# Attention and FFN on one core: VectorE's share of the exponentials as three shifted int16 readings summed by weighted copies of V

## The chip, the cores and the metric

The kernel runs on one core of a Trainium2 chip. Five engines work from queues of their own: PE (TensorE, matmuls), ACT (ScalarE), DVE (VectorE), POOL (GpSimd) and SP (SyncE, which issues DMAs). They meet through semaphores. The metric is the time of one execution in microseconds (us); the kernel before takes 813.2 us, the median of 3 runs between 810.48 and 814.16.

## The reference

```python
xn = layernorm(x)                                   # x: 1 x 2048 x 640
q = (xn @ wq).reshape(1, 2048, 32, 20)              # 32 heads of 20
k, v = xn @ wk, xn @ wv                             # one k and one v for all heads: 2048 x 20
p = softmax(einsum("bhqd,bkd->bhqk", q, k) * 20 ** -0.5)
o = einsum("bhqk,bkd->bhqd", p, v)
out = x + o.reshape(1, 2048, 640) @ wo + silu(xn @ w1) @ w2     # w1: 640 x 1728
```

All is bf16. The 32 x 2048 x 2048 scores need 134 million exponentials; that is the bulk of the work of the engines beside PE.

## The kernel before

**Units, groups, steps.** A unit is one head and one chunk of 512 queries: 128 units. Three units make a group (the last has two), 43 groups. A group takes 16 steps, one for each tile of 128 keys: 688 steps. In step t, `do_S` issues the scores S: three matmuls of 128 keys x 512 queries, side by side in three row tiles of PE (a head has only 20 dimensions), into three PSUM banks. Two sets of three banks alternate, so S of step t+2 waits until the exponentials of step t have been read out. One score block of 512 columns per unit and step is exponentiated:

- ACT takes two or three blocks in one `ACTIVATE` (L735, `exp`).
- In some steps (`want_dve`) DVE takes the third block. The scores come from PE already scaled and offset, so that their integer value is a bf16 bit pattern: `p1` (L749) clamps them and writes int16, Z. Read as bf16, this bit pattern is an exponential that is linear between powers of two. Every four blocks `flush_z` corrects them by three operations over up to 2048 columns: `u` (L800) takes the mantissa, `T1` (L803) multiplies it with Z into Y, `B` (L804) keeps Z's exponent.

The output product P.V follows (`pfn`, L759): 128 keys x 32 columns of V (20 of V, one of ones for the softmax's denominator) against the 512 queries of each unit, in column tiles 0, 1 and 2 of PE side by side. In a DVE step tile 2 takes Y (L765) and tile 3 takes Z (L767); both sums are combined later. At a group's end DVE copies the sums U out of PSUM in fp32r (`Uev`, L821), PE transposes them against a 0/1 matrix `stk` that also adds the tiles up (`UT`, L827), and DVE divides by the denominators (`rcp`, `nrm`).

**Other work** is cut into jobs and put between the steps: q of the next chunk (`q_job`, L867), the FFN's first product (`h_job`, L893, with a tanh on ACT, L901, and a product on DVE, L906), transposes of the attention output (`oT_job`), and the FFN's second product with the output projection (`out_job`: L957 against W2, L962 against wo). In the last chunk the W2 part is made ahead (`dst="yx"`), and the wo part stands behind the last group.

**What sets the order.** The program plans itself while it is built: `Sched.run` and `step` keep an expected time for every engine, and pick for PE a score step, a P.V step or a job matmul; the result is a fixed order for each engine. Where PE is expected to be empty, `fill` puts in matmuls with zeros (L635, L641, L654). `want_dve` gives DVE a block if its backlog is below `DVE_TH`. Changing the numbers changes the whole order.

**The head.** Up to about 60 us x is loaded, normalised (`norm`, into `xn`) and transposed; k, v and the first q are made. `v_job` writes V to SBUF once for four key tiles (L1295). POOL prepares constants.

Of the kernel before, what the change touches and what calls it, by code (L numbers as in the profile page):

```python
# [9 lines left out]
F32R = mybir.dt.float32r  # L10
# [5 lines left out]
P = 128  # L16
# [23 lines left out]
OFF_LO = 53.0  # L40
# [5 lines left out]
ZB = 4  # L46
# [3 lines left out]
PV_PRESS = 9  # L50
DVE_TH = 4.0
# [274 lines left out]
class Builder:  # L326
# [17 lines left out]
    def alloc(self):  # L344
        sb = self.sb
        self.ps = self.stack.enter_context(self.nc.psum_tensor("psall", [P, 8 * BANK], F32))
        self.xnT = sb([P, DC, S], BF16)
        self.w1 = sb([P, DC, F], BF16)
        self.w2 = sb([P, FC, D], BF16)
        self.wq = sb([P, DC, HT * P], BF16)  # L350
        self.wo = sb([P, DC, D], BF16)
        self.kv_st = sb([P, 2, DC, DH], BF16)
        self.wk = sb([P, DC, P], BF16)
        self.kT = sb([P, 2, S], BF16)
        self.v = sb([P, KT, SLOT], BF16)
# [5 lines left out]
        self.stk = sb([P, 64], F32R)  # L361
# [157 lines left out]
    def step(self, now):  # L519
# [17 lines left out]
        for op in list(self.pv_q)[:4]:  # L537
# [3 lines left out]
            if op.kt < KT and self.pro_left:  # L541
# [35 lines left out]
        if choice == "PV":  # L577
            head = self.pv_q[0]
            d = (0.216 if head.mode == "PV" else 0.5) + self.switch(head.mode)
# [4 lines left out]
        if choice == "PV":  # L584
# [4 lines left out]
            op.work = 0.216  # L589
# [108 lines left out]
    def do_S(self, t, now):  # L698
# [55 lines left out]

        def pfn(pe):
            ins = None
            for j in range(na):
                q = j if j < nh - 1 else 2
                ins = pe.matmul(self.bk(UBANK, 0, QW, q * SLOT, (q + 1) * SLOT), self.v[:, kt, :],  # L759
                                self.E[:, (b0 + j) * QW:(b0 + j + 1) * QW],  # L760
                                start=first, stop=last, tile_position=(0, q * SLOT))
            if dv:
                y = self.Y[:, zs, zp * QW:(zp + 1) * QW].bitcast(BF16)
                z = self.Z[:, zs, zp * QW:(zp + 1) * QW].bitcast(BF16)
                pe.matmul(self.bk(UBANK, 0, QW, 64, 96), self.v[:, kt, :], y, start=first, stop=last,  # L765
                          tile_position=(0, 64))
                ins = pe.matmul(self.bk(UBANK, 0, QW, 96, 128), self.v[:, kt, :], z, start=(gd == 0),  # L767
                                stop=(self.last_dve_kt[g] == kt), tile_position=(0, 96))
# [3 lines left out]
        pv.mm = na + (2 if dv else 0)  # L772
# [16 lines left out]

    def flush_z(self):  # L790
# [5 lines left out]
        yk = [("Y", zs, i) for i in range(n)]  # L796
        Z = self.Z[:, zs, 0:n * QW]
        Y = self.Y[:, zs, 0:n * QW]
        w = n * QW
        sc.new("dve", t_dve_4x(w), lambda v: v.tensor_scalar(Y, Z, 0x7F, 0x3F80, ALU.bitwise_and, ALU.bitwise_or),  # L800
               zk, yk, prio=4.0, name="u")
        yb, zb = Y.bitcast(BF16), Z.bitcast(BF16)
        sc.new("dve", t_dve_2x(w), lambda v: v.tensor_tensor(yb, zb, yb, ALU.mult), zk + yk, yk, prio=4.0, name="T1")  # L803
        sc.new("dve", t_dve_4x(w), lambda v: v.tensor_scalar(Z, Z, 0x7F80, None, ALU.bitwise_and), zk, zk, prio=4.0,  # L804
               name="B")
        for i, (t, pv) in enumerate(self.zblocks):
            ks = [("Z", zs, i), ("Y", zs, i)]
            pv.deps |= sc.deps_of(ks, ())
            for k in ks:
                sc.readers[k].append(pv)  # L810
        self.zblocks = []

    def end_group(self, g):
# [16 lines left out]
        op = sc.new("pe", 0.5, ut, [("U", up), ("stk",)], [("UB",)], name=f"UT{g}", mode="M", queue=False)  # L830
# [214 lines left out]
    def prologue(self):  # L1045
# [16 lines left out]
        def load_w(eng, key, pieces, tag, nb):  # L1062
            deps = sc.deps_of((), [tag])
# [26 lines left out]
        load_w("sp", "2", w2p, ("w2",), P * D * 2)  # L1090
# [13 lines left out]
        for a, b_, kk in ((0, 4, 0), (4, 32, 1)):  # L1104
            def padset(g, a=a, b_=b_):
# [15 lines left out]
        pool(0.4, lambda g: g.memset(self.v[:, :, :], 0.0), [], [("v0",)] + [("v", i) for i in range(8)])  # L1121
        pool(0.2, lambda g: g.memset(self.v[:, :, DH:DH + 1], 1.0), [("v0",)],
             [("v0",)] + [("v", i) for i in range(8)])
        wqd = self.wq[:, :, :].rearrange("p c (h j) -> p c h j", j=SLOT)
        wqs = self.wq_st.rearrange("p c (h d) -> p c h d", d=DH)
        pool(0.2, lambda g: g.memset(self.stk[:, :].bitcast(F32), 0.0), [], [("stk",)])
# [3 lines left out]
        self.s21 = self.sb([P, 21], F32)  # L1130
        pool(0.15, lambda g: g.tensor_scalar(self.s21[:, :], self.idf[:, 96:117], 2.0, 0.0, ALU.mult, ALU.add),
             [("idf",)], [("s21",)])
        pool(0.15, lambda g: g.tensor_tensor(self.stk[:, 42:63], self.idf[:, 64:85], self.s21[:, :], ALU.add),
             [("s21",), ("idf",)], [("stk",)])
# [105 lines left out]
        def tr_job(n):  # L1240
# [8 lines left out]
            def consume(b):  # L1249
# [32 lines left out]
        def v_job(n0, n1):  # L1282
# [10 lines left out]
            def consume(b):  # L1293
                sv = self.bk(b, 0, 20 * m).rearrange("p (i d) -> p i d", d=DH)
                sc.new("dve", 0.07 + m * 0.025, lambda v: v.tensor_copy(self.v[:, n0:n1, 0:DH], sv), [("B", b)],  # L1295
                       [(kk, i) for i in range(n0 // 2, n1 // 2) for kk in ("v", "vv")], prio=0.6, name=f"vev{n0}")
# [82 lines left out]
```

## Time and profile before

| | us |
|---|---|
| runs, median of 3 | 813.2 (810.48 to 814.16) |
| the profiled execution | 810.35 |
| its span, first to last instruction | 808.6 |
| mean granted PE clock | 0.99 of full speed |
| instructions | 16175 |

The profile shows the one execution. Its busy times are shares of the span; a group of instructions is one line of the kernel, with its count, its busy time, the mean time of one, and the idle time just ahead of it. Records of one engine can overlap by their start-up, so a mean is somewhat longer than the busy time divided by the count. On PE several tiles work at the same time, and a matmul's record is longer than the distance to the next.

### The profile page before, as it was taken

Reading aid. Unit: us, or ns where it says so; the run is one execution under the profiler, and the core shown is the slowest. Engines: PE = TensorE matmul, PEld = TensorE weight load, DVE = VectorE, ACT = ScalarE, POOL = GpSimd, SP = SyncE. Lnnn points to the kernel's source line nnn. Section 1 sums busy time; section 2 is a strip of 40 time slices with the busy share of each in tenths; the row PEclk is TensorE's granted clock in tenths of the full one; section 3 lists DMA queues with packets and bytes.
Section 4 is the critical chain, followed back from the end, with each engine's and each line's share of the span. In section 5 each row is a group of like instructions: output and inputs, shape, how many; then the busy total and the mean of one; then the engine's idle time right before and its main releaser. Section 6 shows DMA issues by size and latency. Waiting matters only on the chain.

```text
span 808.6 us, 16175 instructions
## 1 busy us (share of the span) xinstructions
PE 756.7 (94%) x6398; PEld 268.9 (33%) x6457; DVE 757.4 (94%) x1286; ACT 756.3 (94%) x776; POOL 25.0 (3%) x69
## 2 busy tenths in 40 slices
PE   8889999899999999999999999998989999999995
PEld 4432232223233333223333433322323333333343
DVE  7439999999999999999999999999999999999996
ACT  6989999999999999999999999999999999999850
POOL 4700000000000000000000000000000000000000
PEclk9999999999999999999999999999999999999999
DMA  9500000000000000000000001000000010000000
GB/s 291 176 1 1 2 2 1 2 1 1 1 2 17 19 17 17 2 1 1 2 1 1 18 17 34 1 1 1 2 1 2 17 34 18 1 1 2 1 2 33
DMA packets 13067, 15.02 MB, mean 19 GB/s; under 512 B 3200, under 2 KB 12352, under 8 KB 12992
## 3 DMA queue, kind: packets, MB, share of 16 engines
q1 hardware_dynamic: 11680, 13.93, 5.3%
q8 instruction: 52, 0.85, 0.4%
q10 hardware_dynamic: 1312, 0.05, 0.1%
q14 instruction: 23, 0.19, 0.1%
HBM read 11.36 MB, written 2.62 MB: 17 GB/s over the span
## 4 chain that ended last, share of the span: by engine, by line
PE 42%; DVE 25%; ACT 23%; issue 6%; POOL 1%; DMA 0%; DVEq 0%; ACTq 0%; POOLq 0%
ACT sbt L735 21%; PE psall L717 13%; DVE sbt L749 10%; PE psall L759 10%; PE psall L957 8%; DVE sbt L803 5%; PE psall L962 2%; DVE sbt L800 2%; PE psall L893 2%; ACT sbt L901 2%; DVE sbt L804 2%; PE psall L827 2%; PE psall L641 1%; DVE sbt L906 1%; PE psall L867 1%
## 5 line engine op out<-in xcount | busy, mean ns | idle before, releaser
L735 ACT ACTIVATE sbt<-psall 128x1024 bf16<-128x1024 f32 (+2 forms) x688 | 724.1, 1196 | 24.8 <-PE psall L717 22.0
L749 DVE TENSOR_SCALAR sbt<-psall 128x512 int16<-128x512 f32 x499 | 333.3, 684 | 10.9 <-PE psall L717 9.3
L717 PE MATMUL psall<-sbt 32*128 32x512 bf16 x2048 | 269.6, 386 | 27.1 <-ACT sbt L735 18.3
L759 PE MATMUL psall<-sbt 128*32 128x512 bf16 x1549 | 200.7, 386 | 2.7 <-DVE sbt L856 1.0
L765 PE MATMUL psall<-sbt 128*32 128x512 bf16 x499 | 155.8, 384 | 0.0
L803 DVE TENSOR_TENSOR sbt<-sbt 128x2048 bf16<-128x2048 bf16 (+3 forms) x140 | 153.9, 1102 | 0.8
L717 PEld LDWEIGHTS psall<-sbt 32*128 32x128 bf16 x2048 | 69.5, 91 | 248.4 <-ACT sbt L735 104.6
L767 PE MATMUL psall<-sbt 128*32 128x512 bf16 x499 | 149.5, 384 | 0.0
L800 DVE TENSOR_SCALAR sbt<-sbt 128x2048 int16<-128x2048 int16 (+3 forms) x140 | 87.2, 629 | 1.2
L804 DVE TENSOR_SCALAR sbt<-sbt 128x2048 int16<-128x2048 int16 (+3 forms) x140 | 87.6, 627 | 0.2
L957 PE MATMUL psall<-sbt 128*128 128x320 bf16 x448 | 87.0, 303 | 0.3 <-DVE sbt L971 0.2
L759 PEld LDWEIGHTS psall<-sbt 128*32 128x32 bf16 x1549 | 53.5, 95 | 87.3 <-issue 46.2
L893 PE MATMUL psall<-sbt 128*128 128x512 bf16 (+1 forms) x245 | 78.4, 395 | 3.8 <-issue 2.9
L641 PE MATMUL psall<-sbt 128*32 128x512 bf16 (+8 forms) x190 | 53.7, 355 | 0.0
L957 PEld LDWEIGHTS psall<-sbt 128*128 128x128 bf16 x448 | 35.6, 97 | 45.3 <-issue 30.9
L867 PE MATMUL psall<-sbt 128*128 128x512 bf16 x142 | 43.6, 384 | 3.4 <-issue 1.0
L654 PE MATMUL psall<-sbt 128*128 128x512 bf16 (+6 forms) x156 | 42.6, 385 | 3.2 <-POOL sbt L1101 1.4
L906 DVE SCALAR_TENSOR_TENSOR sbt<-sbt,psall 128x512 bf16<-128x512 bf16 (+1 forms) x56 | 38.3, 683 | 2.0 <-ACT sbt L901 1.3
L901 ACT ACTIVATE sbt<-psall 128x512 bf16<-128x512 f32 (+1 forms) x56 | 38.8, 694 | 0.0
L765 PEld LDWEIGHTS psall<-sbt 128*32 128x32 bf16 x499 | 38.2, 95 | 0.0
L767 PEld LDWEIGHTS psall<-sbt 128*32 128x32 bf16 x499 | 35.4, 94 | 0.1
L962 PE MATMUL psall<-sbt 128*128 128x320 bf16 x160 | 30.8, 302 | 2.8 <-DVE sbt L924 2.1
(87 smaller groups left out, 349.1 us busy)
## 6 DMA issues: line engine op xcount, KB each, us to landing
sbt<-in_A_x_dram SPq DMA_DIRECT2D x32, 160.0 KB, 2.8
out_dram<-sbt SPq DMA_DIRECT2D x16, 160.0 KB, 1.8
sbt<-in_B_w_dram SPq DMA_DIRECT2D x5, 432.0 KB, 6.3
sbt<-in_B_w_dram SPq DMA_DIRECT2D x13, 160.0 KB, 4.6
sbt<-in_A_wo_dram SPq DMA_DIRECT2D x5, 160.0 KB, 6.2
sbt<-in_A_wq_dram SPq DMA_DIRECT2D x5, 140.0 KB, 3.5
sbt<-in_A_wq_dram SPq DMA_DIRECT2D x1, 100.0 KB, 3.5
sbt<-in_B_w_dram SPq DMA_DIRECT2D x1, 80.0 KB, 4.5
```

The source lines that it names most:

```text
L641: return pe.matmul(self.bk(UBANK, 0, n, 0, 32), self.zero[:, 0:32], self.zero[:, 0:n], start=False, stop=False, tile_position=(0, 0), skip ...
L717: ins = pe.matmul(self.bk(par3 + j), self.kT[r:r + SLOT, kk, kt * P:(kt + 1) * P], self.qT[r:r + SLOT, h // 4, (x // H) % 2, :], start=Tru ...
L735: return a.activation(self.E[:, b0 * QW:(b0 + na) * QW], self.ps[:, par3 * BANK:(par3 + na) * BANK], AF.Exp, scale=ACT_SCALE)
L749: return v.tensor_scalar(self.Z[:, zs, zp * QW:(zp + 1) * QW], self.bk(bb), 0.0, ZMAX, ALU.max, ALU.min)
L759: ins = pe.matmul(self.bk(UBANK, 0, QW, q * SLOT, (q + 1) * SLOT), self.v[:, kt, :], self.E[:, (b0 + j) * QW:(b0 + j + 1) * QW], start=fir ...
L765: pe.matmul(self.bk(UBANK, 0, QW, 64, 96), self.v[:, kt, :], y, start=first, stop=last, tile_position=(0, 64))
L767: ins = pe.matmul(self.bk(UBANK, 0, QW, 96, 128), self.v[:, kt, :], z, start=(gd == 0), stop=(self.last_dve_kt[g] == kt), tile_position=(0 ...
L800: sc.new("dve", t_dve_4x(w), lambda v: v.tensor_scalar(Y, Z, 0x7F, 0x3F80, ALU.bitwise_and, ALU.bitwise_or), zk, yk, prio=4.0, name="u")
L803: sc.new("dve", t_dve_2x(w), lambda v: v.tensor_tensor(yb, zb, yb, ALU.mult), zk + yk, yk, prio=4.0, name="T1")
L804: sc.new("dve", t_dve_4x(w), lambda v: v.tensor_scalar(Z, Z, 0x7F80, None, ALU.bitwise_and), zk, zk, prio=4.0, name="B")
L893: return pe.matmul(self.bk(b, 0, QW, 0, rows), self.w1[:, k, fk * P:fk * P + rows], self.xnT[:, k, c * QW:(c + 1) * QW], start=(k == 0), s ...
L957: return pe.matmul(self.bk(b, 0, 320), self.hT[0:rows, fk, i * P:(i + 1) * P], self.w2[0:rows, fk, e0:e0 + 320], start=(m == 0), stop=(m = ...
```

## The change

The three flush operations give way to two additions: `y0 = Z + 43` and `y1 = Z + 86` in int16 (`PH` holds the shifts and weights). Z, y0 and y1, all read as bf16, are multiplied with copies of V scaled by 1, 0.805 and 0.625, and PSUM sums the three. V is kept in five forms: three weights, and the third weight once more in two halves that fit into the free columns of tiles 0 and 1. A DVE step's P.V slot takes two ACT blocks, z in tile 2 and y0 in tile 3. The third readings y1 are collected in steps of their own, named PT, up to three blocks to a slot (tiles 2, 3, and 0 with 1). Three blocks make a flush instead of four (`ZB`), and `DVE_TH` and `PV_PRESS` have new values. U is written in bf16 and transposed in bf16. W2's tile now also holds `xn`, so W2's load waits until the transposes have read `xn`.

```diff
-OFF_LO = 53.0
+OFF_LO = 45.0
+PH = ((0, 1.0), (43, 0.8046875), (86, 0.625))
-ZB = 4
+ZB = 3
-PV_PRESS = 9
-DVE_TH = 4.0
+PV_PRESS = 12
+DVE_TH = 2.6
@@ alloc
-        self.v = sb([P, KT, SLOT], BF16)
+        self.v = sb([P, 5, KT, SLOT], BF16)
-        self.Y = sb([P, NZ, ZB * QW], I16)
-        self.U = sb([P, 2, QW], F32R)
+        self.Y = sb([P, NZ, 2, ZB * QW], I16)
+        self.U = sb([P, 2, QW], BF16)
-        self.xn = sb([P, 4, D], BF16)
+        self.xn = self.w2[:, 0:4, :]
@@ do_S, pfn
             if dv:
-                pe.matmul(self.bk(UBANK, 0, QW, 64, 96), self.v[:, kt, :], y, start=first, stop=last,
-                          tile_position=(0, 64))
-                ins = pe.matmul(self.bk(UBANK, 0, QW, 96, 128), self.v[:, kt, :], z, start=(gd == 0),
-                                stop=(self.last_dve_kt[g] == kt), tile_position=(0, 96))
+                self.pv_mm(pe, 2, 0, kt, z, first, last)
+                ins = self.pv_mm(pe, 3, 1, kt, y, gd == 0, False)
@@ flush_z
-        sc.new("dve", t_dve_4x(w), lambda v: v.tensor_scalar(Y, Z, 0x7F, 0x3F80, ALU.bitwise_and, ALU.bitwise_or),
-               zk, yk, prio=4.0, name="u")
-        yb, zb = Y.bitcast(BF16), Z.bitcast(BF16)
-        sc.new("dve", t_dve_2x(w), lambda v: v.tensor_tensor(yb, zb, yb, ALU.mult), zk + yk, yk, prio=4.0, name="T1")
-        sc.new("dve", t_dve_4x(w), lambda v: v.tensor_scalar(Z, Z, 0x7F80, None, ALU.bitwise_and), zk, zk, prio=4.0,
-               name="B")
+        for k in range(2):
+            sc.new("dve", t_dve_4x(w), lambda v, k=k: v.tensor_scalar(
+                self.Y[:, zs, k, 0:n * QW], Z, float(PH[k + 1][0]), None, ALU.add), zk,
+                [("Y", zs, k, i) for i in range(n)], prio=4.0 + 0.1 * k, name=f"y{k}")
...
+            def th(pe, q, x=x, kt=kt):
+                if q >= 2:
+                    return self.pv_mm(pe, q, 2, kt, x, False, False)
+                self.pv_mm(pe, 0, 3, kt, x, False, False)
+                return self.pv_mm(pe, 1, 4, kt, x, False, False)
...
+            def fn(pe, part=part):
+                ins = None
+                for q, x in zip((2, 3, 0), part):
+                    ins = x[0](pe, q)
+                return ins
+            op = sc.new("pe", 0.3, fn, [x[1] for x in part], [], name="PT", mode="PV", queue=False)
@@ end_group
-        op = sc.new("pe", 0.5, ut, [("U", up), ("stk",)], [("UB",)], name=f"UT{g}", mode="M", queue=False)
+        op = sc.new("pe", 0.28, ut, [("U", up), ("stk",)], [("UB",)], name=f"UT{g}", mode="M", queue=False)
@@ prologue
-        load_w("sp", "2", w2p, ("w2",), P * D * 2)
+        def load_w2():
+            load_w("sp", "2", w2p, ("w2",), P * D * 2, [("xn", i) for i in range(4)])
-        pool(0.4, lambda g: g.memset(self.v[:, :, :], 0.0), [], [("v0",)] + [("v", i) for i in range(8)])
+        pool(0.9, lambda g: g.memset(self.v[:, :, :, :], 0.0), [], [("v0",)] + [("v", i) for i in range(8)])
...
@@ tr_job, consume
+                if n == NT - 1:
+                    load_w2()
@@ v_job, consume
-                sc.new("dve", 0.07 + m * 0.025, lambda v: v.tensor_copy(self.v[:, n0:n1, 0:DH], sv), [("B", b)],
-                       [(kk, i) for i in range(n0 // 2, n1 // 2) for kk in ("v", "vv")], prio=0.6, name=f"vev{n0}")
+                for k, o, a, b_ in ((0, 0, 0, DH), (1, 0, 0, DH), (2, 0, 0, DH), (3, 21, 0, 11), (4, 21, 11, DH)):
+                    sc.new("dve", 0.07 + m * (b_ - a) / 960.0, lambda v, k=k, o=o, a=a, b_=b_: v.tensor_scalar(
+                        self.v[:, k, n0:n1, o:o + b_ - a], sv[:, :, a:b_], PH[min(k, 2)][1], None, ALU.mult),
+                        [("B", b), ("v0",)], [(kk, i) for i in range(n0 // 2, n1 // 2) for kk in ("v", "vv")], prio=0.6,
+                        name=f"vev{n0}")
```

The planner makes another order of it. In the whole program DVE's clamps L749 go from 499 to 545; ACT's `exp` over three blocks from 186 to 139, over two from 489 to 537; on PE 202 PT steps are new, and the matmuls with zeros go from 362 to 182.

DVE in the middle of the program, before (L749 clamp, L800 `u`, L803 `T1`, L804 `B`, L821 U's copy, L977 an output):

```order
L749 TENSOR_SCALAR sbt<-psall 128x512 x2
L800 TENSOR_SCALAR sbt<-sbt 128x2048
L749 TENSOR_SCALAR sbt<-psall 128x512
L803 TENSOR_TENSOR sbt<-sbt 128x2048
L749 TENSOR_SCALAR sbt<-psall 128x512
L977 SCALAR_TENSOR_TENSOR sbt<-psall,sbt 128x320
L749 TENSOR_SCALAR sbt<-psall 128x512
L821 CAST sbt<-psall 128x512
L749 TENSOR_SCALAR sbt<-psall 128x512
L804 TENSOR_SCALAR sbt<-sbt 128x2048
```

And after, also near a group's end (L807 both additions, L869 U's copy, L888 and L904 the division, L927 a q):

```order
L749 TENSOR_SCALAR sbt<-psall 128x512 x2
L807 TENSOR_SCALAR sbt<-sbt 128x1536 x2
L749 TENSOR_SCALAR sbt<-psall 128x512 x3
L869 CAST sbt<-psall 128x512
L927 TENSOR_SCALAR sbt<-psall,sbt 128x512
L749 TENSOR_SCALAR sbt<-psall 128x512
L888 RECIPROCAL sbt<-psall 128x12
L807 TENSOR_SCALAR sbt<-sbt 128x1536
L904 TENSOR_TENSOR sbt<-psall,sbt 128x4x60
```

The clamps stand between two additions instead of three operations, one of them a product of two tensors.

PE at steps 410 to 413, before (L717 S, L759/L765/L767 P.V, L957 and L962 `out_job`, L635 zeros):

```order
L717 MATMUL psall<-sbt 128x512 x3
L635 MATMUL psall<-sbt 128x320 x2
L717 MATMUL psall<-sbt 128x512 x3
L827 MATMUL psall<-sbt 128x64 x4
L957 MATMUL psall<-sbt 128x320 x2
L717 MATMUL psall<-sbt 128x512 x3
L957 MATMUL psall<-sbt 128x320 x5
```

And after, around the same steps (all P.V and PT matmuls are L795 now; L1005 and L1010 are `out_job`):

```order
L717 MATMUL psall<-sbt 128x512 x3
L795 MATMUL psall<-sbt 32x512 x8
L717 MATMUL psall<-sbt 128x512 x3
L795 MATMUL psall<-sbt 32x512 x12
L717 MATMUL psall<-sbt 128x512 x3
L1010 MATMUL psall<-sbt 128x320 x2
L717 MATMUL psall<-sbt 128x512 x3
L795 MATMUL psall<-sbt 32x512 x15
```

The runs of 12 and 15 hold P.V steps of up to four matmuls with a PT step among them; no zeros stand here any more.

PE at the end, before (the last P.V steps, the last of the eight W2 jobs, the transposes of `oT_job` L917, `UT` L827, then wo's products):

```order
L717 MATMUL psall<-sbt 128x512 x2
L957 MATMUL psall<-sbt 128x320 x9
L759 MATMUL psall<-sbt 32x512
L765 MATMUL psall<-sbt 32x512
L767 MATMUL psall<-sbt 32x512
```

```order
L957 MATMUL psall<-sbt 128x320 x14
L759 MATMUL psall<-sbt 32x512
L765 MATMUL psall<-sbt 32x512
L767 MATMUL psall<-sbt 32x512
L759 MATMUL psall<-sbt 32x512 x2
L917 MATMUL psall<-sbt 128x128 x4
L827 MATMUL psall<-sbt 128x64 x4
L962 MATMUL psall<-sbt 128x320 x8
```

And after, from the last scores on (L941 `h_job`, L641 zeros, L875 `UT`, L965 `oT_job`):

```order
L717 MATMUL psall<-sbt 128x512 x2
L795 MATMUL psall<-sbt 32x512 x5
L641 MATMUL psall<-sbt 32x512
L641 MATMUL psall<-sbt 32x352
L795 MATMUL psall<-sbt 32x512 x8
L1005 MATMUL psall<-sbt 128x320 x14
L795 MATMUL psall<-sbt 32x512 x12
L1005 MATMUL psall<-sbt 128x320 x7
L875 MATMUL psall<-sbt 128x64 x4
L1005 MATMUL psall<-sbt 128x320 x91
L965 MATMUL psall<-sbt 128x128 x4
```

Of the 112 products of the eight W2 jobs, 89 stood among the last 24 score steps and 23 behind them; now all 112 stand behind them, and `UT` stands among them.

More of the change, by code (lines that the diff above doesn't have):

```diff
@@ L540, in step @@
             r = sc.ready(op)
-            if op.kt < KT and self.pro_left:
+            if op.kt < KT:
                 r = max(r, self.reads_ready([("vv", op.kt // 2)]))
@@ L578, in step @@
             head = self.pv_q[0]
-            d = (0.216 if head.mode == "PV" else 0.5) + self.switch(head.mode)
+            d = (0.216 if head.mode == "PV" else head.dur) + self.switch(head.mode)
         else:
@@ L588, in step @@
             op.dur = d
-            op.work = 0.216
+            op.work = min(op.work, 0.216)
             self.u_open = op.kt < KT - 1
@@ L753, in do_S @@
         last = kt == KT - 1
+        if dv:
+            y = self.Y[:, zs, 0, zp * QW:(zp + 1) * QW].bitcast(BF16)
+            z = self.Z[:, zs, zp * QW:(zp + 1) * QW].bitcast(BF16)
+        thirds = []
         def pfn(pe):
@@ L758, in pfn @@
                 q = j if j < nh - 1 else 2
[L759 to L761 removed]
+                ins = self.pv_mm(pe, q, 0, kt, self.E[:, (b0 + j) * QW:(b0 + j + 1) * QW], first, last)
             if dv:
[L763 to L768 removed]
+                self.pv_mm(pe, 2, 0, kt, z, first, last)
+                ins = self.pv_mm(pe, 3, 1, kt, y, gd == 0, False)
+            if first and nh == 2:
+                ins = self.pv_mm(pe, 1, 0, kt, self.zero[:, 0:QW], True, False)
+            for x in thirds:
+                ins = x(pe, 3)
             return ins
@@ L771, in do_S @@
                     name=f"PV{t}", mode="PV", queue=False)
-        pv.mm = na + (2 if dv else 0)
+        pv.after = None if dv or nh < 3 or gd == 0 else thirds
+        pv.mm = na + (2 if dv else 0) + (1 if first and nh == 2 else 0)
         pv.kt = kt
@@ L810, in flush_z @@
                 sc.readers[k].append(pv)
+            x = self.Y[:, zs, 1, i * QW:(i + 1) * QW].bitcast(BF16)
+            kt = t % KT
+            def th(pe, q, x=x, kt=kt):
[3 more added lines that the diff above has]
+                return self.pv_mm(pe, 1, 4, kt, x, False, False)
+            ts.append((th, ("Y", zs, 1, i), kt))
+        first = self.zblocks[0][1]
+        tail = None
+        if self.pv_wait[-1][0].kt == KT - 1 and self.pv_wait[-1][0] is not self.zblocks[-1][1]:
+            tail = self.pv_wait.pop()
+        seen = False
+        hosts = []
+        for op, _ in self.pv_wait:
+            seen = seen or op is first
+            if seen and op.after is not None and not op.after and op.kt < KT:
+                hosts.append(op)
+        while ts and hosts and len(ts) % 3 == 1:
+            th, key, kt = ts.pop()
+            op = hosts.pop()
+            op.after.append(th)
+            op.mm += 1
+            op.deps |= sc.deps_of([key], ())
+            sc.readers[key].append(op)
+        while ts:
+            part = ts[:3]
+            ts = ts[3:]
+            def fn(pe, part=part):
[4 more added lines that the diff above has]
+            op = sc.new("pe", 0.3, fn, [x[1] for x in part], [], name="PT", mode="PV", queue=False)
+            op.mm = len(part) + len(part) // 3
+            op.kt = part[-1][2]
+            op.na = 0
+            op.after = None
+            self.pv_wait.append((op, False))
+        if tail is not None:
+            self.pv_wait.append(tail)
         self.zblocks = []
@@ L1060, in load_x, with load_w @@
             op.inc_no = 1
-        def load_w(eng, key, pieces, tag, nb):
-            deps = sc.deps_of((), [tag])
+        def load_w(eng, key, pieces, tag, nb, over=()):
+            deps = sc.deps_of((), [tag] + list(over))
             for f in pieces:
```

29 lines of the change are left out of this document (16 added, 13 removed).

## The prediction

> **What bounds the kernel now.** I read the busy shares first, then the exponentials' own lines, the stages, and last who waits for whom.
>
> ```profile
> PE 756.7 (94%) x6398; PEld 268.9 (33%) x6457; DVE 757.4 (94%) x1286; ACT 756.3 (94%) x776; POOL 25.0 (3%) x69
> PE 42%; DVE 25%; ACT 23%; issue 6%; POOL 1%; DMA 0%; DVEq 0%; ACTq 0%; POOLq 0%
> ```
>
> Three engines stand at 94%, and the chain (second row) runs through all three. The average doesn't decide; the stages do. Columns: stretch, its length, busy time of PE, weight loads, DVE, ACT and POOL, granted clock, DMA share, GB/s.
>
> ```profile
> 0.00:20.00 20.00, 17.70 (x92) 8.08 (x94) 14.89 (x57) 12.69 (x25) 8.85 (x37) 1.00 0.91 290
> 20.00:60.00 40.00, 34.82 (x331) 16.04 (x332) 15.92 (x38) 37.61 (x34) 16.17 (x33) 0.96 0.27 91
> 60.00:757.00 697.00, 661.01 (x5635) 224.68 (x5689) 683.08 (x1099) 686.74 (x695) 0.00 (x0) 0.99 0.02 7
> 757.00:786.50 29.50, 29.31 (x233) 11.87 (x232) 28.86 (x62) 17.83 (x24) 0.00 (x0) 1.00 0.00 1
> 786.50:792.40 5.90, 5.85 (x50) 2.79 (x50) 4.49 (x12) 1.41 (x2) 0.00 (x0) 1.00 0.01 3
> 792.40:808.60 16.20, 8.05 (x64) 5.41 (x64) 10.15 (x25) 0.00 (x0) 0.00 (x0) 0.91 0.12 41
> 266.00:311.80 45.80, 45.26 (x413) 16.69 (x413) 45.45 (x78) 44.55 (x44) 0.00 (x0) 1.00 0.08 23
> 174.60:221.30 46.70, 44.42 (x366) 13.80 (x368) 44.58 (x73) 45.11 (x46) 0.00 (x0) 0.96 0.00 1
> ```
>
> From 60 to 757 us ACT is busy 686.7 of 697 us, DVE 683.1. PE's 661 contains its fillers. From 757 to 786.5 the last scores are interleaved with the last FFN products: PE and DVE are full, and ACT only 17.8 of 29.5. Behind that comes a tail of 16.2 us in which nothing is full. The waits (us, times, longest) agree:
>
> ```profile
> PEld psall L717 <- ACT sbt L735: 104.6, 251, 1.6
> PEld psall L717 <- DVE sbt L749: 57.9, 149, 0.8
> ACT sbt L735 <- PE psall L717: 22.0, 39, 2.2
> ```
>
> The scores (L717) wait for a score bank, mostly for ACT's exp to read it, next for DVE's clamp; ACT itself waits 22 us in all. So ACT sets the pace up to 757 us, DVE is 0.5% behind it, and PE has slack that it fills with zeros.
>
> **The change part by part.** The rows that price it (count | busy, mean ns):
>
> ```profile
> L735 ACT ACTIVATE sbt<-psall 128x1024 bf16<-128x1024 f32 x489 | 480.3, 1093 | 12.8 <-PE psall L717 11.7 <-PE psall L767 0.4
> L735 ACT ACTIVATE sbt<-psall 128x1536 bf16<-128x1536 f32 x186 | 275.9, 1508 | 4.1 <-PE psall L717 2.5 <-PE psall L759 1.5
> L749 DVE TENSOR_SCALAR sbt<-psall 128x512 int16<-128x512 f32 x499 | 333.3, 684 | 10.9 <-PE psall L717 9.3
> L803 DVE TENSOR_TENSOR sbt<-sbt 128x2048 bf16<-128x2048 bf16 (+3 forms) x140 | 153.9, 1102 | 0.8
> L800 DVE TENSOR_SCALAR sbt<-sbt 128x2048 int16<-128x2048 int16 (+3 forms) x140 | 87.2, 629 | 1.2
> L804 DVE TENSOR_SCALAR sbt<-sbt 128x2048 int16<-128x2048 int16 (+3 forms) x140 | 87.6, 627 | 0.2
> L800 DVE TENSOR_SCALAR sbt<-sbt 128x1536 int16<-128x1536 int16 x8 | 4.4, 556 | 0.0
> L800 DVE TENSOR_SCALAR sbt<-sbt 128x1024 int16<-128x1024 int16 x13 | 5.2, 424 | 0.0
> L800 DVE TENSOR_SCALAR sbt<-sbt 128x512 int16<-128x512 int16 x9 | 2.6, 291 | 0.1
> L803 DVE TENSOR_TENSOR sbt<-sbt 128x1536 bf16<-128x1536 bf16 x8 | 7.6, 955 | 0.1
> ```
>
> *ACT.* The order has 545 clamped blocks instead of 499. A block of 512 costs ACT 1508 - 1093 = 415 ns, so ACT loses 46 x 0.415 = 19.1 us, all of it before the last 43 steps, where both orders have 35 such blocks. Calls and tanh stay: 756.3 - 19.1 = 737.2 us.
>
> *DVE.* Out go the three flush operations, 153.9 + 87.2 + 87.6 = 328.7 us. In come 46 clamps at 0.668 (333.3 / 499), 30.7 us, and 404 int16 additions: 314 over 1536, 58 over 1024, 32 over 512. No addition on int16 in SBUF stands in the trace. Nearest is the bitwise operation of the same engine, width and type: 314 x 0.556 + 58 x 0.424 + 32 x 0.291 = 208 us. The other end is the two-operand product, at about twice that: 314 x 0.955 is 300, about 353 in all. I take 208, since that row differs in the operation alone. DVE: 757.4 - 328.7 + 30.7 + 208 = 667 us, 90 less than now; it stops being second in line, and its longest operation falls from 1.1 to 0.56 us, so clamps wait less. The Trainium skill ("VectorE: DVE Perf Modes", What auto-detection actually checks) says that the rate is chosen by element size, step and memory, not by the operation, so an int16 addition would run like the bitwise row; by that rule the term is the 208 us above, otherwise 353. The bitwise rows fit it (1536 cost 556 ns, where the product costs 955), but no row here shows an addition.
>
> *PE.* These rows price slots, mode changes (the chain: start, us) and transposes (start, us):
>
> ```profile
> 759.86 0.32 PE psall L759 x2
> 760.18 0.21 PE psall L759 x3
> 792.38 0.40 PE L917 MATMUL psall<-sbt 128*128 128x128 bf16 x4
> 793.12 0.63 PE L827 MATMUL psall<-sbt 128*128 128x64 f32 x4 [0.34 <-DVE sbt L821]
> 795.78 1.26 PE L962 MATMUL psall<-sbt 128*128 128x320 bf16 x8 [0.69 <-DVE sbt L924]
> L957 PE MATMUL psall<-sbt x448: 299/299/315, 241.8 to 791.5; 128*128 128x320 bf16 x139, 64*128 64x320 bf16 x11
> ```
>
> A P.V step, up to four matmuls in four column tiles, takes 0.215 us; a change of kind adds 0.11. A clamped step still has four matmuls (z and y0 replace y and z). New are 202 PT slots, 43.4 us, and 68 more changes of kind, 7.5 us. U in bf16 makes the 43 UT transposes cost like L917's, 0.40 for 0.63: -9.9 us (bounds 0 and -27). Fillers fall from 362 to 182, their columns from 163584 to 85792: at 0.215 per 512, 68.7 to 36.0 us. So 41 us of work replace 33 us of filler, in a kernel that ACT makes 19 us shorter. That is tight. The tightest stretch now is steps 215 to 257 (266 to 311.8 us): 43 scores, 45 P.V and 5 q slots at 0.215, 95 FFN products at 0.136, 3 UT and 92 changes make 44.9 us of 45.8, no filler, and it kept ACT's pace (44.55 busy). After, the same steps hold 43 scores, 42 P.V, 12 PT, 10 q, 86 products, 2 UT and 92 changes: 23.0 + 11.7 + 0.8 + 10.1 = 45.6, where ACT, with three blocks fewer, wants 45.8 - 1.2 = 44.6. I put 1 us on PE for it (0 to 10 with its like).
>
> *Last steps.* The planner now leaves all eight last FFN jobs behind the final scores. Before, 23 of the 112 products stand there. So ACT stays the bound up to the last exp: 737.2 busy, idle 9.7 before 60 us (60 - 12.69 - 37.61), 10.3 up to 757 and 0.3 beyond, 1 for the stretch above and 1 for the head below: it ends at 759.5, against 788.0 now (756.3 + 9.7 + 10.3 + 11.7). The last scores are issued two exps and a tanh earlier, 757.5. Then PE alone: 7 P.V and 3 PT slots 2.2, 112 products at 0.137 ((1.26 - 0.30) / 7) 15.3, scores, UT and changes 1.0, fillers 0.4: 18.9 us, to 776.4, where now 792.4 stands. The tail of 16.2 loses UT's 0.5, since UT now runs among the products: end at 792.1.
>
> *Head.*
>
> ```profile
> L1295 DVE CAST sbt<-psall x4: 241/242/242, 36.7 to 53.4; 128x80 bf16<-128x80 f32 x4
> 47.22 11.88 ACT L735 ACTIVATE sbt<-psall 128x1536 bf16<-128x1536 f32 x10 [1.46 <-PE psall L759]
> 4.35 0.52 POOL L1121 MEMSET sbt<- 128x512 bf16 x1
> 16.22 0.26 POOL L1201 TENSOR_SCALAR sbt<-sbt 128x6 f32<-128x6 f32 x1 [9.45 <-DVE sbt L1166]
> ```
>
> V is written five times: each of four V jobs holds P.V back 4 x 0.242 = 1 us longer, while ACT already waited 1.46 us for P.V once. DVE is idle there (15.9 of 40 busy); ACT feels one such delay, +1 us (0 to 3.9). POOL's memset is five times as wide, 2 us more, and six small ones: all inside its 9.45 us wait. W2's 14 loads wait for the last transposes (about 45 us) because xn now lies in W2; their first reader comes at 241.8, and nothing behind them on SP's queue is due before 221 us. Hidden. U's cast is PSUM-bound either way: nothing.
>
> *Sum.* Span 808.6 - 19.1 (ACT) + 1 + 1 - 11.4 (ACT's late idle) + 13.0 (18.9 for 5.9 behind the last scores) - 0.5 and a rest of -0.5 (scores ahead of the last exp) = 792.1. The profiled execution took 810.35, 1.75 outside its span, so 793.8; the median shown, 813.2, is 2.85 above that one: 796.6.
>
> **Rivals.** (a) *The additions run at half rate or less: slower.* At the product's price DVE rises to 757.4 - 328.7 + 30.7 + 353 = 812 us; with its present 51 us of idle time that is a span of 863, 868 by the median. It decides from about 0.75 us per 1536 on, where DVE's work passes ACT's. For it: no such row. Against: the bitwise row. 5%.
> (b) *PE becomes the bound.* If half of the 202 PT slots land in steps where ACT can't wait, 100 x 0.215 = 21 us come back: 813 + 5 = 818 by the median. For it: the tight stretch. Against: PE at 98% there already held ACT's pace, and by the same count every other stretch of 43 steps but one leaves PE 1.5 us or more. A quarter of the slots, 11 us, gives 807. 8% for a loss of all the gain or more.
> (c) *PE's clock drops as fillers go.* The granted clock is 0.96 in the emptiest stretch, 174.6 to 221.3, which has 52 fillers; 4% of 46.7 is 1.9 us. Ten such stretches would give the 19 us back: 815. Against: work and filler in those steps make 37 us of 44 after, 38 of 47 before, and all others are fuller. 3%. The Trainium skill ("TensorE: Matmul & The Clock Gate", Part 1: The HAM clock gate) has an idle window of about 3.4 us halve the clock; by that rule removing filler is a risk, and the 0.96 agrees with it.
> (d) *More gain.* With DVE early, ACT's 10 us of idle time up to 757 shrink to 3: 789.6. That is 794.2 by the median, and 789 where ACT's waits at the very start go too. 15%.
>
> **How the numbers follow.** My case has 69%: 796.6, own range 791 to 807 (the lower offset of the profiled run below, a quarter of the PT slots above). Faster: it and (d), 0.84. Within 0.5% (809.1 to 817.3, about what the runs' spread of 810.5 to 814.2 lets a measurement tell from no change): (c) and 5 of (b)'s 8, 0.08. Slower: (a) and the rest of (b), 0.08. The range is 786 to 809: below lies (d) with the lower offset of the profiled run, above lie (a), (c) and the hard end of (b).
>
> **What would show it.** ACT's blocks of 1536 fall to 139 and its busy time to 737; L807's additions take 0.56 us per 1536; scores hardly wait for L749; ACT ends near 760 us and PE runs 112 products back to back behind it; PE's fillers halve. Wrong if the additions cost over 0.75 us, or if ACT's idle time before its last exp grows past 35 us, with PE as what it waits for.

## The result and the profile after

The changed kernel takes 793.15 us (median of 4 runs, 791.65 to 794.72), against 813.67 (810.48 to 814.16) for the kernel before on the same chip: a ratio of 0.976, 95% interval 0.972 to 0.979. Forecast were 796.5 us and 786 to 809. The profiled execution took 791.86, its span is 790.0.

The page of the changed kernel, its first part:

```profile
span 790.0 us, 17413 instructions
PE 744.9 (94%) x6965; PEld 252.9 (32%) x7026; DVE 678.1 (86%) x1332; ACT 733.8 (93%) x776; POOL 27.2 (3%) x73
```

DVE is no longer level with the others. Where the 18.6 us of span went is seen by stages. The scores of each step are the same work in both kernels, so I cut both traces at the first weight load of steps 43, 645 and 687 (the last) and of the first output transpose. Columns as in the prediction's table of stretches. Before (its last two stretches stand in the prediction):

```profile
77.70:734.50 656.80, 624.00 (x5328) 212.23 (x5379) 643.14 (x1032) 647.02 (x654) 0.00 (x0) 0.99 0.02 7
734.50:786.50 52.00, 49.95 (x411) 19.34 (x408) 51.36 (x101) 39.85 (x48) 0.00 (x0) 1.00 0.00 1
```

After:

```profile
77.30:710.90 633.60, 607.85 (x5832) 196.27 (x5879) 571.03 (x1076) 623.86 (x649) 0.00 (x0) 1.00 0.03 8
710.90:754.00 43.10, 41.34 (x352) 12.10 (x355) 41.10 (x83) 40.79 (x52) 0.00 (x0) 1.00 0.01 2
754.00:774.05 20.05, 20.05 (x146) 11.42 (x145) 7.40 (x18) 1.76 (x3) 0.00 (x0) 1.00 0.00 1
774.05:790.00 15.95, 7.59 (x61) 4.95 (x60) 9.45 (x22) 0.00 (x0) 0.00 (x0) 0.98 0.12 42
```

| stretch | before | after | difference |
|---|---|---|---|
| up to step 43 | 77.7 | 77.3 | -0.4 |
| steps 43 to 644 | 656.8 | 633.6 | -23.2 |
| steps 645 to 686 | 52.0 | 43.1 | -8.9 |
| last scores to first output transpose | 5.9 | 20.05 | +14.15 |
| tail | 16.2 | 15.95 | -0.25 |
| sum | 808.6 | 790.0 | -18.6 |

In steps 43 to 644 ACT's busy time fell by 23.2 us, as much as the stretch; ACT idles 9.8 us there before and 9.7 after. In the last 43 steps DVE was full before (51.36 of 52.0) and no engine is after. But 89 of the W2 products have also left that stretch, an estimated 12 us of PE at the 0.137 each of the prediction, and are paid behind the last scores: there PE is busy for all of 20.05 us, the other engines for little of it. The groups of instructions:

```profile
L735 ACT ACTIVATE sbt<-psall 128x1024 bf16<-128x1024 f32 (+2 forms) x688 | 703.0, 1173 | 16.3 <-PE psall L717 12.5
L749 DVE TENSOR_SCALAR sbt<-psall 128x512 int16<-128x512 f32 x545 | 365.9, 685 | 47.8 <-PE psall L717 38.1
L807 DVE TENSOR_SCALAR sbt<-sbt 128x1536 int16<-128x1536 int16 (+2 forms) x404 | 196.8, 510 | 2.8 <-PE psall L795 0.4
L807 DVE TENSOR_SCALAR sbt<-sbt 128x1536 int16<-128x1536 int16 x314 | 168.6, 549 | 2.1
L875 PE MATMUL psall<-sbt 128*128 128x64 bf16 x168 | 12.1, 195 | 0.9 <-DVE sbt L869 0.9
```

An int16 addition over 1536 takes 549 ns, the bitwise operation took 556. The waits:

```profile
PEld psall L717 <- ACT sbt L735: 103.4, 263, 0.9
PEld psall L717 <- DVE sbt L749: 54.6, 141, 0.8
DVE sbt L749 <- PE psall L717: 38.1, 91, 1.1
ACT sbt L735 <- PE psall L717: 12.5, 21, 2.6
PEld psall L795 <- DVE sbt L807: 8.5, 32, 0.4
```

Scores wait for ACT as before, and DVE's clamps now wait for scores (38.1 us; 9.3 before). But scores still wait 54.6 us for clamps, hardly less than the 57.9 of before. P.V and PT matmuls (L795) wait 8.5 us for the additions.

### The profile page after: what moved, and what is told of

The parts are those of the page before. It is cut to its first block, busy times and chain, and to the rows that moved or that the text cites. A ratio compares the mean times of both kernels' runs of the same rounds, so it can differ in the third digit from the quotient of the medians.

```text
span 790.0 us, 17413 instructions
## 1 busy us (share of the span) xinstructions
PE 744.9 (94%) x6965; PEld 252.9 (32%) x7026; DVE 678.1 (86%) x1332; ACT 733.8 (93%) x776; POOL 27.2 (3%) x73
## 4 chain that ended last, share of the span: by engine, by line
PE 44%; ACT 34%; DVE 10%; issue 8%; POOL 1%; DMA 0%; DVEq 0%; ACTq 0%; POOLq 0%
ACT sbt L735 31%; PE psall L795 13%; PE psall L717 13%; PE psall L1005 7%; DVE sbt L749 5%; PE psall L941 3%; ACT sbt L949 3%; PE psall L1010 2%; DVE sbt L807 2%; PE psall L915 2%; DVE sbt L954 1%; PE psall L641 1%; PE psall L965 1%; DVE sbt L869 0%; PE psall L875 0%
## 5 line engine op out<-in xcount | busy, mean ns | idle before, releaser
L735 ACT ACTIVATE sbt<-psall 128x1024 bf16<-128x1024 f32 (+2 forms) x688 | 703.0, 1173 | 16.3 <-PE psall L717 12.5
L749 DVE TENSOR_SCALAR sbt<-psall 128x512 int16<-128x512 f32 x545 | 365.9, 685 | 47.8 <-PE psall L717 38.1
L717 PE MATMUL psall<-sbt 32*128 32x512 bf16 x2048 | 268.9, 384 | 17.9 <-ACT sbt L735 12.2
L795 PE MATMUL psall<-sbt 128*32 128x512 bf16 x3296 | 257.1, 384 | 1.6 <-issue 0.8
L807 DVE TENSOR_SCALAR sbt<-sbt 128x1536 int16<-128x1536 int16 (+2 forms) x404 | 196.8, 510 | 2.8 <-PE psall L795 0.4
L717 PEld LDWEIGHTS psall<-sbt 32*128 32x128 bf16 x2048 | 69.6, 91 | 255.3 <-ACT sbt L735 103.4
L795 PEld LDWEIGHTS psall<-sbt 128*32 128x32 bf16 x3296 | 68.9, 95 | 110.3 <-issue 65.0
L941 PE MATMUL psall<-sbt 128*128 128x512 bf16 (+1 forms) x247 | 78.0, 386 | 8.2 <-DVE sbt L954 3.8
L1005 PE MATMUL psall<-sbt 128*128 128x320 bf16 x448 | 82.2, 302 | 0.3 <-DVE sbt L1025 0.3
L1005 PEld LDWEIGHTS psall<-sbt 128*128 128x128 bf16 x448 | 36.6, 97 | 39.7 <-issue 27.6
L1010 PE MATMUL psall<-sbt 128*128 128x320 bf16 x160 | 31.5, 303 | 3.4 <-DVE sbt L972 2.7
L941 PEld LDWEIGHTS psall<-sbt 128*128 128x128 bf16 (+1 forms) x280 | 19.3, 98 | 44.2 <-issue 26.4
L869 DVE CAST sbt<-psall 128x512 bf16<-128x512 f32 (+1 forms) x43 | 29.4, 684 | 2.1 <-PE psall L795 1.9
L641 PE MATMUL psall<-sbt 128*32 128x512 bf16 (+10 forms) x91 | 27.0, 353 | 0.0
L927 DVE TENSOR_SCALAR sbt<-psall,sbt 128x512 bf16<-128x512 f32 x31 | 23.1, 746 | 3.7 <-PE psall L915 3.4
L654 PE MATMUL psall<-sbt 128*128 128x512 bf16 (+2 forms) x84 | 22.6, 396 | 2.2 <-POOL sbt L1151 1.4
```

What stands on the lines that cost most here:

```text
L641: return pe.matmul(self.bk(UBANK, 0, n, 0, 32), self.zero[:, 0:32], self.zero[:, 0:n], start=False, stop=False, tile_position=(0, 0), skip ...
L717: ins = pe.matmul(self.bk(par3 + j), self.kT[r:r + SLOT, kk, kt * P:(kt + 1) * P], self.qT[r:r + SLOT, h // 4, (x // H) % 2, :], start=Tru ...
L735: return a.activation(self.E[:, b0 * QW:(b0 + na) * QW], self.ps[:, par3 * BANK:(par3 + na) * BANK], AF.Exp, scale=ACT_SCALE)
L749: return v.tensor_scalar(self.Z[:, zs, zp * QW:(zp + 1) * QW], self.bk(bb), 0.0, ZMAX, ALU.max, ALU.min)
L795: return pe.matmul(self.bk(UBANK, 0, QW, q * SLOT, (q + 1) * SLOT), self.v[:, w, kt, :], x, start=start, stop=stop, tile_position=(0, q * ...
L807: sc.new("dve", t_dve_4x(w), lambda v, k=k: v.tensor_scalar(self.Y[:, zs, k, 0:n * QW], Z, float(PH[k + 1][0]), None, ALU.add), zk, [("Y", ...
```

## The experiments

Theory: ACT's exps set the pace up to the last scores, and the 46 blocks that DVE takes over are the gain, which the cheaper flush makes possible. Rivals: the gain comes from DVE being less late, from U in bf16, or from the planner's numbers; PE's new work eats it. Spans are of the profiled execution; each version is compared with runs of the kernel before on its own chip (medians 811.3, 810.5 and 811.2 in the three sessions).

**The split of the blocks, alone (`e1_share_before`).**

```diff
+DVE_STEPS = int('7faf7f...', 16)              # the 499 steps of the kernel before
...
     def want_dve(self, t):
+        return bool(DVE_STEPS >> t & 1)
+
+    def want_dve_by_backlog(self, t):
         if self.pro_left or t % KT >= KT - NOD:
             return False
```

> The new kernel, but DVE takes exactly the 499 blocks that it took before (a fixed list of steps in place of the backlog rule), so ACT takes 1549 again. Theory (ACT's stream sets the pace, the 46 blocks are the gain): ACT's exps rise by 19.1 us; 42 of the 112 W2 products stand behind the last scores instead of 112, so part of it is given back at the end: 800 to 806 us, some 9 to 12 slower than the new kernel. Rival (the gain is that DVE is no longer late with its clamps, however the blocks are split): 791 to 795, as the new kernel.

Measured: 801.6 us, ratio to before 0.987 (0.983 to 0.992), inside the theory's 800 to 806. Its first page line and its stretches:

```profile
PE 750.7 (94%) x6901; PEld 254.3 (32%) x6959; DVE 643.5 (81%) x1240; ACT 753.2 (94%) x776; POOL 27.4 (3%) x73
79.00:727.50 648.50, 618.33 (x5787) 199.73 (x5838) 540.75 (x989) 644.98 (x655) 0.00 (x0) 1.00 0.03 7
727.50:773.60 46.10, 45.29 (x392) 15.72 (x393) 40.90 (x86) 38.80 (x47) 0.00 (x0) 1.00 0.01 1
773.60:798.70 25.10, 16.68 (x135) 10.11 (x132) 13.33 (x33) 1.42 (x2) 0.00 (x0) 0.98 0.07 27
```

So the gain has two halves. With the old split the new method already saves 9.9 us of span: 8.3 in steps 43 to 644, where ACT now idles 3.5 us instead of 9.8, and 5.9 in the last 43 steps, less 3.0 behind them and 1.3 in the head. The 46 blocks then bring 14.9 in steps 43 to 644, 3.0 in the last ones and 1.7 in the head, and give 10.9 back behind the last scores (36.0 against 25.1): 8.7 in all. The rival, that only DVE's lateness counts, can hold for the first half at most. That half isn't the cheaper flush alone: U in bf16 is in it too, which by itself takes 6.3 us of span off the old kernel (`e6_before_u_bf16`). How the 9.9 us divide was not tried.

**The split without the cheaper flush (`e2_before_545`).** The same edit in the kernel before, with the 545 steps of the new one.

> The kernel before, with its three flush operations, but DVE takes exactly the 545 blocks that it takes in the new one. Theory: each further block costs DVE 0.67 for the clamp and 0.66 for the flush, 46 x 1.33 = 61 us, and DVE, already at 757 busy, becomes the bound: 757 + 61 + 51 idle = 869 of span, 860 to 880 us. Rival (the split alone gains, the cheaper flush isn't needed): 813 - 19 = 794.

Measured: 851.2 us, ratio 1.048 (1.043 to 1.053). DVE is the fullest engine and the kernel slower by 40 us, though below the 860 to 880 expected:

```profile
PE 793.1 (93%) x6596; PEld 280.2 (33%) x6658; DVE 805.7 (95%) x1401; ACT 744.8 (87%) x776; POOL 25.0 (3%) x69
```

DVE rose by 48 us, not 61, and idles 46 us, where 51 was put. The split alone loses; it needs the rest of the change, the cheaper flush first of all.

**What an addition may cost (`e3_adds_as_products`, `e3b_y1_as_product`).** Both additions, or the second one, become an operation of two SBUF operands:

```diff
-            sc.new("dve", t_dve_4x(w), lambda v, k=k: v.tensor_scalar(
-                self.Y[:, zs, k, 0:n * QW], Z, float(PH[k + 1][0]), None, ALU.add), zk,
...
+            def add(v, k=k):
+                if k in (0, 1):        # e3b: (1,)
+                    z = Z.bitcast(BF16)
+                    return v.tensor_tensor(self.Y[:, zs, k, 0:n * QW].bitcast(BF16), z, z, ALU.max)
+                return v.tensor_scalar(self.Y[:, zs, k, 0:n * QW], Z, float(PH[k + 1][0]), None, ALU.add)
```

> The new kernel in the same planned order, but both additions of a flush are a bf16 product-type operation of two SBUF operands (Z max Z), so that the second and third readings are unshifted; it leaves the shifts out. Its price is that of the removed product: 0.955 for 0.549 us at 1536, over all flushes 147 us more on DVE, 678 to 825. Theory (DVE takes over as the bound once its work passes ACT's 734): 825 + 51 idle = 876 of span, 865 to 885 us. Rival (DVE's 112 idle us take up most of it): 793 to 830.

Measured: 890.9 us, ratio 1.097 (1.093 to 1.102), above both ranges expected. This is rival (a) of the prediction as it would have been: DVE is busy 812.1 us, as (a) had it, but the time is worse than its 868. The half step:

> The new kernel in the same planned order; only the second addition of each flush is replaced by the bf16 operation of two operands (Z max Z), so that the third reading is unshifted; it leaves that shift out. DVE gets 73 us more, 678 to 751, the two readings together 0.75 us per 1536 on average, the point from which the prediction let DVE decide. Theory (slack of DVE up to ACT's 734 is free, the rest is paid): 17 us over at most, 795 to 812. Rival (DVE's price is paid from the first microsecond, at the slope of e3_adds_as_products, 98 for 147 us): 838 to 846.

Measured: 824.7 us, ratio 1.017 (1.014 to 1.020). Neither of its two ranges holds: 63 us more on DVE (678.1 to 741.1) cost 31.5 us by the medians, and the next 71 (to 812.1) cost 66. Its busy times and four of its waits:

```profile
PE 757.2 (92%) x6965; PEld 252.8 (31%) x7026; DVE 741.1 (90%) x1332; ACT 744.8 (90%) x776; POOL 27.3 (3%) x73
PEld psall L717 <- DVE sbt L749: 97.1, 222, 1.4
ACT sbt L735 <- PE psall L717: 31.0, 70, 2.6
PEld psall L795 <- DVE sbt L810: 19.6, 42, 1.1
PEld psall L795 <- DVE sbt L811: 12.6, 37, 0.8
```

Scores wait 97 us for clamps instead of 55, P.V and PT matmuls wait 32 us for the two readings (L810, L811) instead of 8.5, and ACT waits 31 us for scores instead of 12.5. My reading: DVE needs not be full to hold the others. A clamp behind a longer flush frees its bank later, a P.V matmul that waits for a reading holds up the scores behind it in PE's fixed order, and ACT starves for that moment. Which of the two waits costs ACT more was not separated.

**The PT steps (`e4_pt_short`, `e8_pt_short_planned`).** One short matmul in place of the third readings, first in the same order:

```diff
-                for q, x in zip((2, 3, 0), part):
-                    ins = x[0](pe, q)
+                return pe.matmul(self.bk(UBANK, 0, 64, 2 * SLOT, 3 * SLOT), self.v[:, 2, 0, :], self.zero[:, 0:64], ...)
```

> The new kernel in the same planned order, but each of the 202 PT steps is one matmul of 64 zero columns, which leaves the third readings out of the sums: 202 slots of 0.215 shrink to about 0.03, 37 us less on PE. Theory (ACT sets the pace, PE only in steps 172 to 257 and at the end): 3 to 7 us come back, 786 to 790. Rival (PE has become the bound): 20 us or more, 773 or less. Second rival (PE's slots are all hidden): 793.

Measured: 789.2 us, ratio 0.973 (0.968 to 0.977): inside the theory's range, 3.4 us of span below the new kernel. The interval overlaps the new kernel's 0.972 to 0.979, so the second rival, that these slots are all hidden, isn't excluded. Then the planner is told that a PT step takes 0.03:

```diff
-            d = (0.216 if head.mode == "PV" else head.dur) + self.switch(head.mode)
+            d = (0.03 if head.name == "PT" else 0.216 if head.mode == "PV" else head.dur) + self.switch(head.mode)
```

> As e4_pt_short (each PT step one matmul of 64 zero columns, the third readings left out of the sums), but the planner knows that a PT step is short. It then puts none of the 112 W2 products behind the last scores (112 in the new kernel) and gives DVE 559 blocks (545). Theory (PE's PT slots are not paid where they stand, but at the end, in the products that they push behind the last scores): 18 us of tail and 6 of ACT less, some of it back in the last 43 steps: 770 to 780. Rival (the PT slots cost only what e4 showed, 3 to 4 us): 786 to 791.

Measured: 774.0 us, ratio 0.954 (0.951 to 0.957), as the theory had it. Its stretches:

```profile
80.60:709.40 628.80, 604.27 (x5508) 199.58 (x5557) 583.99 (x1103) 621.13 (x658) 0.00 (x0) 1.00 0.03 8
709.40:754.80 45.40, 45.21 (x407) 17.94 (x407) 41.13 (x86) 36.99 (x44) 0.00 (x0) 1.00 0.01 1
754.80:772.20 17.40, 9.70 (x84) 5.44 (x83) 11.70 (x30) 1.42 (x2) 0.00 (x0) 0.97 0.11 39
```

The last scores come at 754.8, in the new kernel at 754.0. The gain lies behind them, 17.4 us for 36.0. So PT's 43 us of PE are not free. They take the room that the planner would have given to the W2 products, and these stand at the end, where nothing covers them. The new plan also gives DVE 14 blocks more, and ACT is busy 6.3 us less (727.5); that part of the 17.8 us of span was not separated.

**U in bf16 alone (`e6_before_u_bf16`).**

```diff
-        self.U = sb([P, 2, QW], F32R)
-        self.stk = sb([P, 64], F32R)
+        self.U = sb([P, 2, QW], BF16)
+        self.stk = sb([P, 64], BF16)
...
-        op = sc.new("pe", 0.5, ut, ...
+        op = sc.new("pe", 0.28, ut, ...
```

> The kernel before with one part of the change alone: U and its 0/1 matrix in bf16, UT planned at 0.28 for 0.5 us; still 499 blocks and three flush operations. Theory: PE loses 43 x 0.23 to 0.34 = 10 to 15 us of work, but ACT and DVE, which set the pace, lose nothing: 0 to 4 us faster than before, 807 to 813. Rival (UT is on the path of every group): 10 us or more faster, 801 or less.

Measured: 805.9 us, ratio 0.993 (0.990 to 0.996): 4.6 us faster, a little more than expected. Here too it lies at the end (15.5 us behind the last scores instead of 22.1, since the plan puts all W2 products before them); steps 43 to 644 take 655.0 for 656.8.

**The planner's numbers alone (`e7_before_numbers`).**

```diff
-ZB = 4
-PV_PRESS = 9
-DVE_TH = 4.0
+ZB = 3
+PV_PRESS = 12
+DVE_TH = 2.6
```

> The kernel before, three flush operations and all, with the planner's new numbers alone (ZB 3, DVE_TH 2.6, PV_PRESS 12). The plan then gives DVE 443 blocks for 499. Theory: ACT gets 56 x 0.415 = 23 us more, and 48 fewer products stand at the end: 820 to 836. Rival (the gain is in the planner's numbers): 790 to 800.

Measured: 811.0 us, ratio 1.000 (0.998 to 1.001). The numbers alone gain nothing, but 20 us of loss didn't come either:

```profile
78.70:748.50 669.80, 638.03 (x5317) 214.72 (x5368) 618.34 (x1078) 666.02 (x659) 0.00 (x0) 0.99 0.02 7
748.50:791.90 43.40, 43.21 (x368) 17.07 (x366) 39.12 (x78) 40.08 (x43) 0.00 (x0) 1.00 0.01 2
791.90:809.00 17.10, 10.14 (x85) 5.46 (x84) 12.19 (x31) 1.48 (x2) 0.00 (x0) 0.91 0.11 38
```

ACT works 19.0 us more in steps 43 to 644 and idles 6 less, so these take 13.0 us longer; the last 43 steps, where DVE is no longer full, take 8.6 less, and what stands behind them 5.0 less. The expectation counted the blocks and the products at the end, and left out that ACT would idle less and that the last 43 steps shrink when DVE isn't full in them (39.12 of 43.4). A slower stream of scores leaves PE and DVE more time for their work before its end.

**No fillers (`e5_no_fill`).** `fill` returns at once after the first scores.

> The new kernel without matmuls of zeros from the first scores on: 139 of 182 fall away, 43 stay in the head; the plan is else nearly the same (548 blocks on DVE, 99 W2 products behind the last scores). Theory (ACT sets the pace and PE's clock holds, since PE has work in most of every stretch): 789 to 796. Rival (c) of the prediction (without fillers the granted clock falls in the emptier stretches): a mean clock under 0.98 and 798 or more.

Measured: 789.8 us, ratio 0.973 (0.970 to 0.975), not told apart from the new kernel's 0.976. The clock did fall:

```profile
20.00:80.00 60.00, 47.98 (x445) 18.77 (x446) 33.55 (x76) 53.64 (x50) 15.56 (x32) 0.80 0.21 64
```

The granted clock is 0.80 from 20 to 80 us. It is 0.50 from 21.3 to 31.5, from 48.6 to 62.2 and, behind the head, from 222.7 to 232.9. Step 43 comes at 80.1 instead of 77.3. Steps 43 to 644 take 2.1 us less than in the new kernel, the last ones 0.4, and what stands behind the last scores 1.8, about what 13 products fewer there would give; the plan is not quite the same. So a price of the lower clock can't be read from the total alone. The Trainium skill ("TensorE: Matmul & The Clock Gate", Part 1: The HAM clock gate) says that an idle window of about 3.4 us halves the clock. The trace agrees in kind: in the 3.4 us ahead of the three drops PE is busy for 40%, 42% and 56% by its records, so PE need not be empty for it.

**Going further (`f2_last_step_575`, `f1_last_step_557`).** DVE may also take a block in a group's last step, where PT then closes the group, with other planner's numbers.

```diff
-NOD = 1
+NOD = 0
-            op = sc.new("pe", 0.3, fn, [x[1] for x in part], [], name="PT", mode="PV", queue=False)
+            op = sc.new("pe", 0.3, fn, [x[1] for x in part], [("UB",)] if ends else [], name="PT", mode="PV",
+                        queue=False)
-            op.kt = part[-1][2]
+            op.kt = KT - 1 if ends else part[-1][2]
```

> A version that goes further the same way: DVE may also take a block in the last step of a group (PT steps then close the group), and the planner's numbers let it take 575 blocks for 545 (DVE_TH 2.84, PV_PRESS 15, other PACE, ZWAIT 4). Theory: ACT loses 30 x 0.415 = 12.5 us, PE gains 12 PT slots, 112 W2 products still stand behind the last scores: 780 to 787. Rival (PE takes over once ACT is eased): 790 to 796.

> The milder form of f2_last_step_575: the last step of a group may go to DVE, 557 blocks (DVE_TH 2.68, PV_PRESS 14, S_LEAD 0.59, other PACE), 98 W2 products behind the last scores. Against f2 ACT has 18 x 0.415 = 7.5 us more and the tail 2 us less. Theory (time = ACT's stream up to the last score plus the products behind it): 787 to 792. Rival (PE's work sums to the time, blocks moved at the end are neutral): 782 to 786, as f2.

Measured: 784.4 us, ratio 0.965 (0.962 to 0.969), with 575 blocks, and 785.1, ratio 0.968 (0.964 to 0.971), with 557. Both beat the new kernel. The first page lines, f1 and f2:

```profile
PE 740.7 (95%) x6974; PEld 251.4 (32%) x7038; DVE 688.2 (88%) x1356; ACT 728.5 (93%) x776; POOL 27.3 (3%) x73
PE 743.2 (95%) x7006; PEld 253.5 (32%) x7066; DVE 701.8 (90%) x1386; ACT 722.7 (92%) x776; POOL 27.4 (3%) x73
```

The step from 557 to 575 takes 5.8 us off ACT and nothing off the time: f1's rival held, not its theory; f2's time lies in its theory's range. At this point moving blocks off ACT shortens the stream of scores a little and lengthens what PE has to do behind it: in f2 the last scores come at 746.8 instead of 747.9, and the rest takes 35.7 us instead of 33.4. How much of the 8 to 9 us against the new kernel is the last step and how much the other planner's numbers was not taken apart.

## Why the prediction was right

The time came 3.4 us under the forecast, well inside its range, and by the path that it gave. Of these 3.4 us 2.1 are span (790.0 for 792.1): the last scores came 3.5 earlier, the work behind them took 1.15 and the tail 0.25 longer. The rest is the distance from the profiled span to the median, put at 4.6 and here 3.15; that part is luck. By the prediction's own steps:

- *ACT, 19.1 us less, the pace up to the last scores.* Right, and in size too. `e1_share_before` and the new kernel differ in the 46 blocks and the order that follows from them, and ACT's busy time falls by 19.4 us between them (753.2 to 733.8). Another 3.1 us (756.3 to 753.2) went while the blocks stayed where they were; the forecast hadn't that, and its cause is open. So ACT stands at 733.8, not 737.2, and the last scores came at 754.0 instead of 757.5. ACT's idle time up to its last exp was put at 22.3 us and is 22.0.
- *DVE's price.* The additions were to cost 208 us by the bitwise row and cost 196.8; the clamps 364 and cost 365.9. The Trainium skill's rule ("VectorE: DVE Perf Modes", What auto-detection actually checks), which put the addition level with the bitwise operation, agrees with 549 ns against 556. DVE's total is 678.1, not 667. The busy times of the rows overlap those of their neighbours, and a sum of them can't be read as DVE's time. Counting each of the trace's records only from the end of the one before it, the old flush is 299.4 us and not 328.7, the additions are 178.0 and not 208, the clamps rise by 36.0 and not 30.7, and all else rises by 6.1, 3.5 us of it the V copies that this sum left out. Two errors of 30 us cancelled, by luck.
- *"Clamps wait less"* was wrong: scores wait 54.6 us for them, 57.9 before. What went away is DVE's own fullness.
- *The tight stretch, 1 us for PE.* Steps 172 to 257 took 92.9 us, 2.5 more than before, though DVE has six blocks more there. The PT slots are 0.9 of it at most (`e4_pt_short` has 92.1 there). ACT waits twice for over 2 us, each time behind a run of P.V matmuls that followed on a run of products:

```profile
254.63 32.47 ACT L735 ACTIVATE sbt<-psall 128x1536 bf16<-128x1536 f32 x32 [2.32 <-PE psall L717]
289.67 16.27 ACT L735 ACTIVATE sbt<-psall 128x1536 bf16<-128x1536 f32 x16 [2.58 <-PE psall L717]
252.78 1.48 PE L795 MATMUL psall<-sbt 128*32 128x512 bf16 x24
```

- *The last steps.* Forecast were 18.9 us of PE alone behind the last scores, measured 20.05; each job of 14 products takes a little more than its slots:

```profile
760.40 13.74 PE psall L1005 x91
```

  91 products at 0.137 would be 12.5 us. The tail was 15.95 for 15.7. The transposes UT, priced at 0.40 us by L917's row, took 0.28.
- *The head.* ACT waits 3.3 us for P.V (1.46 before), 1.9 more where 1 was put, and step 43 still comes 0.4 earlier. The granted clock from 20 to 60 us was 1.00 in this execution and 0.96 in the one before, which the forecast didn't count. POOL's wider memset took 2.23 us and was hidden, as was W2's later load.
- *Rival (a)* fell because the addition has the bitwise operation's price. But its turning point was wrong. At 0.75 us per 1536 on average DVE has 741.1 us, 7 more than the 733.8 of the new kernel's ACT, and by "decides ... where DVE's work passes ACT's" some 7 us would be lost; the kernel is 31.5 us slower (33.7 of span) and already behind the kernel before. That step of the rival failed: DVE's longer operations also delay scores and P.V, at a price beyond its surplus.
- *Rival (b)* was put at steps where ACT can't wait. That price is 3.4 us of span (`e4_pt_short`), not clear of noise; but with the slots gone from the plan too the span falls by 17.8 (`e8_pt_short_planned`), most of it at the end, which the sum had as its +13.0 and didn't connect with them.
- *Rival (c)* is right that the clock falls without fillers and wrong on the time. *Rival (d)* didn't happen: ACT's idle time in steps 43 to 644 is 9.7 us, 9.8 before. Its 794.2 was a slip besides: 789.6 is 796.6 less 7, by the median already, and the 4.6 from span to median was added a second time.

## What to carry to other kernels

When three engines stand at 94%, cut both traces at the same pieces of work and ask in each stretch which engine is full; here it was ACT for most of the time, DVE (with PE close to it) in the last 43 steps, PE behind them, and the parts of the change acted in different ones. Work put on an engine with slack isn't free if the order is made by a planner: it may be paid far from where it stands, in the jobs that lose their place. An engine whose results release a buffer or feed the next engine can cost more than its surplus over the fullest one, so don't price an added operation there by the idle share alone: here 63 us more cost 31.5, and the next 71 cost 66.

## What was unexpected of the hardware

Raising DVE's work from 678 to 741 us, 7 us above the 734 that ACT has in the new kernel, cost 31.5 us. And 139 matmuls of zeros, put there to keep PE busy, could go without a measurable loss, in a plan that is nearly the same, though the granted clock stood at 0.50 for 34 us in three stretches.
